# Cached attention beside a small feed-forward on one core: a weight block loaded a round later, half of the last V in the key buffers, and the products of two heads moved ahead of the last maximum

## The chip, the cores and the metric

The kernel runs on one core of a Trainium2 chip. The metric is the device time of one execution in microseconds, the median of several. Five engines run side by side and meet only at semaphores: TensorE (PE in the profile), VectorE (DVE), ScalarE (ACT), GpSimd (POOL, nearly unused here) and SyncE (SP), which here does nothing but issue transfers from DRAM to the on-chip memory. A transfer that SP issues must first wait until its destination buffer is free, and SP issues in program order: while it waits, every later transfer waits behind it.

## The reference

Two rows of input x (B = 2, D = 448) go through two branches, which are mixed by a gate. Everything is f32.

```python
g = sigmoid((x * gate_w).sum(-1))
q = (x @ wq)                                  # 16 heads of 256, one query row per batch entry
p = softmax(q . k_cache * 256 ** -0.5)        # 4096 keys for each head and batch entry
a = (p @ v_cache) @ wo                        # back to 448
h = relu(x @ w1 + b1) ** 2                    # 1792 wide
b = h @ w2 + b2
out = g * a + (1 - g) * b
```

Nearly all bytes are k_cache and v_cache, 134 MB each. The weights are wq 7.3 MB, wo 7.3 MB, w1 and w2 3.2 MB each. Each byte is used once.

## The kernel before

**Rounds.** The 32 pairs of a batch entry and a head are worked off in 16 rounds, `rounds[i] = (b, n)` (L129): round i takes batch entry b and the two heads 2n and 2n+1, 64 partitions for each head, 64 keys in each partition. Round 15 is the last. Heads 12 and 13 are rounds 12 and 13, heads 14 and 15 are rounds 14 and 15.

**Buffers.** There are three ring buffers of 4.2 MB (`slot`, L69) and one wide buffer of 8.4 MB (`wide_slot`, L72). A round's keys come in two halves, each in a ring buffer (`load_k`, L138; the text calls the halves k5_0 and k5_1 for round 5). A round's values fill the wide buffer (`load_v`, L144; v5 for round 5). Weight blocks take a whole ring buffer, however small they are: w1 in round 1, the first two chunks of w2 (`load_w2_early`, 0.46 MB), the four groups of wo (`load_wo`, 1.84 MB each; called wo0 to wo3) and the other twelve chunks of w2 (`load_w2_late`, 2.75 MB in four pieces).

**What a round does.** DVE multiplies the half of the keys by the query in place (`times_q`, L295) and adds up along the head (`row_sums`, L300), for both halves; `rest(i)` is that for all but the first 16 columns. Then comes the round's maximum (L304, turned across partitions by a product on PE, L308, and read back at L314), ACT takes the exponentials (L319), and PE multiplies them with V (`values`, L345, 64 matmuls a round). While PE does this, DVE is already at the next round's keys.

**What sets the order.** It is the order of the program, engine by engine (`manual_schedule`, L67). SP's issues stand at the head of each round: the round's V, then weight blocks, then the second half of the next round's keys and the first half of those after it (L423 to L438). V waits for the wide buffer, that is for the end of the products of the round before. A ring buffer comes free when `row_sums` has read a half of keys, or when the last product with a weight block is done.

**Units of heads.** Four heads share an accumulator. When a unit is done (rounds 3, 7 and 11), its sum is read by ACT (`take`, L355), turned by PE (`turn`, L373) and multiplied with its group of wo (`project`, L386); round 3 also multiplies the two early chunks of w2 (L464). The last four heads form two units of two heads. Their products with wo3 (`late_wo`, L394) and those with the late chunks of w2 (`late_w2`, L398) go into a second accumulator, all through the helper at L391.

**The end.** In the last round V comes in four pieces (`V_CUTS`), and PE multiplies each as it lands; the `late_wo` of heads 12 and 13 stand between these pieces (L477 to L483). Then follow `take` and `turn` of the last unit, the late chunks of w2 and heads 14 and 15, one reading by ACT (L491) and two small stores.

Of the kernel before, what the change touches and what calls it, by code (L numbers as in the profile page):

```python
# [16 lines left out]
def kernel(  # L17
# [14 lines left out]
    nc = tc.nc  # L32
    P = 128
    B, H, S, DH = k_cache.shape
# [7 lines left out]
    NK = S // PH  # L42
    J = NK // 2
# [8 lines left out]
    DQ = D // 4  # L52
    WH = 2
    W2_CUTS = (4, 8, 11)
    V_CUTS = (32, 48, 56)
    LEAD = 4
    LEAD2 = 16
    scale = DH ** -0.5
# [10 lines left out]
    def slot(name):  # L69
        return ring.tile([P, J * DH], F32, name=name, tag="ring")  # L70

    def wide_slot(name):  # L72
        return wide.tile([P, NK * DH], F32, name=name, tag="wide")
# [10 lines left out]
    def load_w1():  # L84
        t = slot("w1")[:, :D * F // P]
        nc.sync.dma_start(t, w1.rearrange("(r k) (s n) -> (r k s) n", k=XR, s=2).rearrange(
            "(p k) n -> p (k n)", k=XR))
        return t
# [11 lines left out]
    def load_w2_early():  # L100
        tv = w2_slot(0, WH)
        nc.sync.dma_start(tv, w2_v[:, :WH, :])

    def load_w2_late():
        tv = w2_slot(WH, FC)
        at = [0, *W2_CUTS, FC - WH]
        for lo, hi in zip(at, at[1:]):
            nc.sync.dma_start(tv[:, lo:hi, :], w2_v[:, WH + lo:WH + hi, :])  # L108
# [9 lines left out]
    def load_wo(g):  # L118
        t = slot(f"wo{g}")
        tv = t[:, :HJ * D]  # L120
        if g < NG - 1:
            nc.sync.dma_start(tv, wo_g[g])
            wo_sb[g] = tv.rearrange("p (j n) -> p j n", j=HJ)
        else:
            nc.sync.dma_start(tv.rearrange("p (h k) -> p h k", h=HG), wo_v[:, g * HG:(g + 1) * HG, :])
            wo_sb[g] = tv.rearrange("p (h j n) -> p h j n", h=HG, j=NJ)
# [3 lines left out]
    last = len(rounds) - 1  # L130

    def of_round(src, i):
        b, n = rounds[i]
        return src[b, 2 * n:2 * n + 2].rearrange("h (p j) d -> (h p) j d", p=PH)
# [3 lines left out]
    def load_k(i, half):  # L138

        t = slot(f"k{i}_{half}").rearrange("p (j d) -> p j d", d=DH)  # L140
        nc.sync.dma_start(t, of_round(k_cache, i)[:, half * J:(half + 1) * J, :])
        kts[i, half] = t

    def load_v(i, cuts=()):  # L144
        t = wide_slot(f"v{i}").rearrange("p (j d) -> p j d", d=DH)
        at = [0, *cuts, NK]
        for lo, hi in zip(at, at[1:]):
            nc.sync.dma_start(t[:, lo:hi, :], of_round(v_cache, i)[:, lo:hi, :])  # L148
        return t


    wq_t = load_wq()
# [139 lines left out]
    def times_q(i, half, lo, hi):  # L292

        kt = kts[i, half][:, lo:hi, :]
        nc.vector.tensor_tensor(kt, kt, q_sb[i].unsqueeze(1).to_broadcast([P, hi - lo, DH]), op=ALU.mult)  # L295

    def row_sums(i, half):
        if half == 0:
            s_t[i] = work.tile([P, NK], F32, name=f"s{i}", tag="s")
        nc.vector.tensor_reduce(s_t[i][:, half * J:(half + 1) * J], kts[i, half], axis=AX.X, op=ALU.add)  # L300

    def maximum(i):
        m = work.tile([P, 1], F32, name=f"m{i}", tag="m")
        nc.vector.tensor_reduce(m, s_t[i], axis=AX.X, op=ALU.max)  # L304
        mt = ps.tile([P, 512], F32, name=f"mt{i}", tag="sm")
        for k in range(2):
            at = slice(k * PH, (k + 1) * PH)
            nc.tensor.matmul(mt[at, :PH], m.to_broadcast([P, PH]), ident[:, at], start=True, stop=True)  # L308
        return mt

    def softmax(i, mt):
        b, n = rounds[i]
        nb = work.tile([P, 1], F32, name=f"nb{i}", tag="nb")
        nc.vector.tensor_reduce(nb, mt[:, :PH], axis=AX.X, op=ALU.max, negate=True)  # L314
        u, k = unit_of[2 * n]
        for e in range(2):
            at = slice(e * PH, (e + 1) * PH)
            c = B * (k + e) + b
            nc.scalar.activation(pw[k, b][at, :, 2 * c:2 * c + 2], s_t[i][at].rearrange("p (m s) -> p m s", s=2), AF.Exp,  # L319
                                 bias=nb[at], accum_out=rs_t[u % 2][at, c:c + 1])  # L320

    def sums(u):
        sm = ps.tile([P, 512], F32, name=f"sum{u}", tag="sm")
        n = B * len(units[u])
        nc.tensor.matmul(sm[:, :n], ones_pp, rs_t[u % 2][:, :n], start=True, stop=True)  # L325
        return sm

    def norm(u, sm):
        n = len(units[u])
        rc = work.tile([P, n, B], F32, name=f"rc{u}", tag="rc")  # L330
        nc.vector.reciprocal(rc, sm[:, :B * n].rearrange("p (k b) -> p k b", b=B))
        nc.vector.tensor_tensor(rc, rc, gP[:, 0, :].unsqueeze(1).to_broadcast([P, n, B]), op=ALU.mult)
        rl = work.tile([P, n * B, 2], F32, name=f"rl{u}", tag="rl")
        nc.vector.tensor_tensor(rl, m16[:, :4 * n].rearrange("p (c s) -> p c s", s=2),
                                rc.rearrange("p k b -> p (k b)").unsqueeze(2).to_broadcast([P, n * B, 2]), op=ALU.mult)
        rl_t[u] = rl

    def values(i, vt, lo=0, hi=NK // 2):
        b, h = rounds[i]
        u, k = unit_of[2 * h]  # L340
        n = len(units[u])
        po = po_bufs[u % 2]
        for m in range(lo, hi):
            r = 32 * (m % 4)
            nc.tensor.matmul(po[r:r + 4 * n, :], pw[k, b][:, m, :4 * n], vt[:, 2 * m:2 * m + 2, :].rearrange("p j d -> p (j d)"),  # L345
                             start=(k == 0 and b == 0 and m < 4), stop=(k == n - 2 and b == B - 1 and m >= NK // 2 - 4))
# [37 lines left out]
    def project(g):  # L384
        for j in range(HJ):
            nc.tensor.matmul(acc[:, :D], oT[g][:, j, :], wo_sb[g][:, j, :], start=False,  # L386
                             stop=(g == NG - 2 and j == HJ - 1))

    def late(lt, rhs, start=False, stop=False):
        for k in range(4):  # L390
            nc.tensor.matmul(fin[32 * k:32 * k + B, :DQ], lt, rhs[:, k * DQ:(k + 1) * DQ], start=start, stop=stop)  # L391

    def late_wo(h):
        u, k = unit_of[h]  # L394
        for j in range(NJ):
            late(oT[u][:, j, B * k:B * k + B], wo_sb[NG - 1][:, h % HG, j, :])
# [13 lines left out]
    def rest(i):  # L410
        times_q(i, 0, LEAD2, J)
        row_sums(i, 0)
        times_q(i, 1, 0, J)
        row_sums(i, 1)
# [3 lines left out]
    for i, (b, n) in enumerate(rounds):  # L418
        u, k = unit_of[2 * n]
        done = b == B - 1 and k == len(units[u]) - 2  # L420


        vt = load_v(i, V_CUTS if i == last else ())  # L423
        if i == 1:
            w1_t = load_w1()
        if i == 3:
            load_w2_early()
        if done and u < NG - 1:
            load_wo(u)
        if i == last - 1:  # L430
            load_wo(NG - 1)
        if i == last:
            load_w2_late()
        if i < last - 1:
            load_k(i + 1, 1)
            load_k(i + 2, 0)
        if i == last - 2:
            load_k(last, 1)  # L438

        mt = maximum(i)  # L440
        if i < last:
            times_q(i + 1, 0, 0, LEAD)
        softmax(i, mt)
        if i < last:
            times_q(i + 1, 0, LEAD, LEAD2)
        if done:
            norm(u, sums(u))
        if i == last:
            break
        values(i, vt)  # L450


        if done:
            take(u)
            turn(u)
            if u < NG - 1:
                project(u)
        if i == 1:
            ffn_hidden(w1_t)
        if i == 2:  # L460
            pt = ffn_turn()
        if i == 3:
            for c in range(WH):
                nc.tensor.matmul(acc[:, :D], hT[:, c, :], w2_sb[c], start=False, stop=False)  # L464
        if i + 2 <= last:
            make_q(i + 2)
        if i == last - 3:

            ya = const.tile([B, D], F32, name="ya")
            nc.scalar.activation(ya, acc[:, :D], AF.Copy)  # L470
            late(ident[:B, :B], ya, start=True)
        rest(i + 1)
        if i == 2:
            ffn_square(pt)


    p1, p2, p3 = (c // 2 for c in V_CUTS)  # L477
    values(last, vt, 0, p1)
    values(last, vt, p1, p2)
    late_wo(H - 4)  # L480
    values(last, vt, p2, p3)
    late_wo(H - 3)
    values(last, vt, p3, NK // 2)  # L483
    take(NG)
    turn(NG)
    late_w2(0, W2_CUTS[0])
# [35 lines left out]
```

## Time and profile before

| what | value |
|---|---|
| median of 3 runs | 702.95 us (702.36 to 703.0) |
| the profiled execution's own time | 703.78 us |
| its span, first to last instruction | 702.0 us |
| bytes read from DRAM | 289.56 MB, 412 GB/s over the span |
| DVE busy | 571.9 us (81%) |
| PE busy | 240.4 us (34%) |
| granted TensorE clock, mean | 0.653 |

The span lies 1.78 us below the profiled execution's own time, which in turn lies 0.83 us above the median of the runs. In the profile, one row of the timeline is a group of like instructions: its start, its duration, the engine, the line, and in brackets the idle time of the engine before it and what ended it. A row of the chain of waits is a link of the chain that ended last: start, duration, and what took it; for a transfer it runs from the issue to the landing. A row of the windows gives, for a stretch of the span, the busy time of PE, of its weight loads (PEld), of DVE, ACT and POOL, then the granted clock, the busy share of the DMA engines and the GB/s that they moved.

### The profile page before, as it was taken

To read this page: it belongs to the slowest core of one execution; us is meant where nothing else is said; L and a number is where in the kernel's file an instruction comes from. 1 tells how busy PE (TensorE), PEld (TensorE's weight loads), DVE (VectorE), ACT (ScalarE), POOL (GpSimd) and SP (SyncE) were. 2 spreads that over 40 slices of the span, in tenths; PEclk is the share of its full clock that TensorE was granted. 3 is DMA by queue.
4 is the path that set the end of the run, shared out by engine and by line. 5 is a ranking of instruction groups with operands and counts; after the bars stand their busy time and mean duration, and the time that the engine had idled before them with its cause. 6 is when DMAs were issued, how large, how long until landed. Compare 5 with 4: busy or idle time off the path is not lost.

```text
span 702.0 us, 3763 instructions
## 1 busy us (share of the span) xinstructions
PE 240.4 (34%) x1618; PEld 82.8 (12%) x1618; DVE 571.9 (81%) x171; ACT 35.5 (5%) x110; POOL 0.7 (0%) x6
## 2 busy tenths in 40 slices
PE   2501408018086050321407440230507532240436
PEld 1100102004041010000103110000103100010013
DVE  3299997897948929979895989989795998989940
ACT  0100000100010000000001000000001000000000
POOL 0000000000000000000000000000000000000000
PEclk9955757656567565565757666565757657575678
DMA  9999999999975999999989999999999999999786
GB/s 413 399 444 422 471 418 415 429 436 450 399 311 209 418 445 448 390 451 415 474 388 434 471 395 446 420 439 428 440 437 420 441 426 433 429 426 447 300 361 275
DMA packets 9500, 289.79 MB, mean 413 GB/s; under 512 B 1158, under 2 KB 1292, under 8 KB 2316
## 3 DMA queue, kind: packets, MB, share of 16 engines
q1 hardware_dynamic: 9320, 289.54, 96.2%
q8 instruction: 12, 0.20, 0.1%
q10 hardware_dynamic: 164, 0.02, 0.0%
q14 instruction: 4, 0.03, 0.0%
HBM read 289.56 MB, written 0.00 MB: 412 GB/s over the span
## 4 chain that ended last, share of the span: by engine, by line
DMA 65%; PE 20%; DVE 12%; ACT 1%; SPq 0%; issue 0%; ACTq 0%
DMA v<-in_A_v_cache_dram 59%; PE po_buf L345 17%; DVE k L295 6%; DVE s L300 6%; DMA w<-in_B_w_dram 4%; DMA wq<-in_A_wq_dram 3%; PE po_buf L215 1%; PE acc L386 1%; PE ot L373 1%; ACT shared L355 0%; SPq L148 0%; PE fin L391 0%; SPq L108 0%; ACT oT L379 0%; PE pq L252 0%
## 5 line engine op out<-in xcount | busy, mean ns | idle before, releaser
L295 DVE TENSOR_TENSOR k<-k,q 128x4096 f32<-128x4096 f32 (+3 forms) x63 | 281.7, 4487 | 95.2 <-DMA k<-in_A_k_cache_dram 76.6
L300 DVE TENSOR_REDUCE s<-k 128x32 f32<-128x8192 f32 x32 | 278.0, 8686 | 1.1
L345 PE MATMUL po_buf<-v,pw 128*16 128x512 f32 (+1 forms) x1024 | 145.5, 730 | 166.1 <-DMA v<-in_A_v_cache_dram 166.1
L308 PE MATMUL mt<-ident,m 128*64 128x64 f32 x64 | 7.7, 335 | 256.4 <-DVE m L304 256.4
L345 PEld LDWEIGHTS po_buf<-v,pw 128*16 128x16 f32 (+1 forms) x1024 | 32.2, 110 | 265.7 <-issue 225.3
L308 PEld LDWEIGHTS mt<-ident,m 128*64 128x64 f32 x64 | 5.1, 204 | 263.9 <-issue 220.7
L319 ACT ACTIVATE pw<-s,nb 64x64 f32<-64x64 f32 x32 | 11.2, 349 | 295.6 <-DVE nb L314 295.2
L386 PE MATMUL acc<-wo,oT 128*2 128x448 f32 x48 | 24.3, 671 | 2.5 <-ACT oT L379 2.5
L373 PE MATMUL ot<-rl,shared 128*128 128x8 f32 x96 | 16.1, 305 | 5.2 <-ACT shared L355 5.2
L255 ACT ACTIVATE q<-pq 128x256 f32<-128x256 f32 x16 | 6.1, 384 | 209.9 <-PE pq L252 209.8
L373 PEld LDWEIGHTS ot<-rl,shared 128*128 128x128 f32 x96 | 15.6, 254 | 8.3 <-ACT shared L355 8.3
L252 PE MATMUL pq<-qs,ident 128*64 128x256 f32 x64 | 10.7, 419 | 0.7 <-ACT qs L241 0.7
L215 PE MATMUL po_buf<-wq,xT 128*4 128x512 f32 x56 | 8.1, 741 | 4.7 <-DMA wq<-in_A_wq_dram 4.7
L355 ACT ACTIVATE shared<-po_buf 128x1024 f32<-128x1024 f32 x6 | 5.8, 1021 | 53.5 <-PE po_buf L345 53.5
L276 PEld LDWEIGHTS pt<-ident,shared 4*128 4x128 f32 x28 | 6.9, 336 | 0.9 <-issue 0.9
L276 PE MATMUL pt<-ident,shared 4*128 4x4 f32 x28 | 7.0, 380 | 0.0
L386 PEld LDWEIGHTS acc<-wo,oT 128*2 128x2 f32 x48 | 4.4, 97 | 20.1 <-issue 17.3
L319 ACT ACTIVATION_READ_ACCUMULATOR pw<-s,nb 64x1 f32 x32 | 5.9, 185 | 0.0
L325 PE MATMUL sum<-rs,ones_pp 128*128 128x8 f32 (+1 forms) x10 | 3.0, 368 | 8.1 <-ACT pw L319 8.1
L215 PE MATMUL ph<-w,xT 128*4 128x448 f32 x28 | 5.4, 539 | 0.0
L252 PEld LDWEIGHTS pq<-qs,ident 128*64 128x64 f32 x64 | 3.3, 138 | 11.7 <-issue 9.8
L314 DVE TENSOR_REDUCE nb<-mt 128x1 f32<-128x64 f32 x16 | 3.5, 218 | 0.7 <-PE mt L308 0.7
(60 smaller groups left out, 54.8 us busy)
## 6 DMA issues: line engine op xcount, KB each, us to landing
k<-in_A_k_cache_dram SPq DMA_DIRECT2D x32, 4096.0 KB, 31.0
wq<-in_A_wq_dram SPq DMA_DIRECT2D x1, 7168.0 KB, 19.5
wo<-in_A_wo_dram SPq DMA_DIRECT2D x4, 1792.0 KB, 29.5
v<-in_A_v_cache_dram SPq DMA_DIRECT2D x1, 4096.0 KB
w<-in_B_w_dram SPq DMA_DIRECT2D x1, 3136.0 KB, 33.2
v<-in_A_v_cache_dram SPq DMA_DIRECT2D x1, 2048.0 KB
v<-in_A_v_cache_dram SPq DMA_DIRECT2D x2, 1024.0 KB, 19.6
w<-in_B_w_dram SPq DMA_DIRECT2D x2, 896.0 KB, 23.0
```

The costliest lines, as they stand in the source:

```text
L215: nc.tensor.matmul(out[32 * g:32 * g + 2 * B, :width], xT[:, half, c].rearrange("p s b -> p (s b)"), t[:, (a * n + g) * width:(a * n + g + ...
L252: nc.tensor.matmul(pq[k * PH:(k + 1) * PH, :DH], ident[:, r:r + 1].to_broadcast([P, PH]), qs[:, k * DH:(k + 1) * DH], start=True, stop=True)
L255: nc.scalar.activation(q_sb[i], pq[:, :DH], AF.Copy)
L276: nc.tensor.matmul(pt[:, c, :], hv[:, c, :], ident[:2 * B, :2 * B], start=True, stop=True)
L295: nc.vector.tensor_tensor(kt, kt, q_sb[i].unsqueeze(1).to_broadcast([P, hi - lo, DH]), op=ALU.mult)
L300: nc.vector.tensor_reduce(s_t[i][:, half * J:(half + 1) * J], kts[i, half], axis=AX.X, op=ALU.add)
L308: nc.tensor.matmul(mt[at, :PH], m.to_broadcast([P, PH]), ident[:, at], start=True, stop=True)
L319: nc.scalar.activation(pw[k, b][at, :, 2 * c:2 * c + 2], s_t[i][at].rearrange("p (m s) -> p m s", s=2), AF.Exp, bias=nb[at], accum_out=rs_ ...
L345: nc.tensor.matmul(po[r:r + 4 * n, :], pw[k, b][:, m, :4 * n], vt[:, 2 * m:2 * m + 2, :].rearrange("p j d -> p (j d)"), start=(k == 0 and ...
L355: nc.scalar.activation(o_w[:, s], po_bufs[u % 2][:, s * DH:(s + 1) * DH].rearrange("r (p j) -> r j p", j=HJ).unsqueeze(2).to_broadcast([P, ...
L373: nc.tensor.matmul(ptv[:, j, :], ov[:, s, j, :], rl_t[u][:, :, s], start=(s == 0), stop=(s == 1))
L386: nc.tensor.matmul(acc[:, :D], oT[g][:, j, :], wo_sb[g][:, j, :], start=False, stop=(g == NG - 2 and j == HJ - 1))
```

## The change

Three things change.

1. `load_w2_early` and the products of its two chunks move from round 3 to round 4. In round 3 wo0 now follows V directly.
2. The last V is loaded by a function of its own. Its first half goes into a ring buffer (`va`), its second half into the second half of the wide buffer (`vb`), in pieces of 16, 8 and 8 columns. As a buffer of the ring goes to `va`, the late chunks of w2 get the next one.
3. The `late_wo` of heads 12 and 13 move from between the pieces of the last V to the end of round 14's products, ahead of the last round's row sums and maximum in the program.

```diff
-    V_CUTS = (32, 48, 56)
+    V_CUTS = (48, 56)
...
-    def load_v(i, cuts=()):
+    def load_v(i):
         t = wide_slot(f"v{i}").rearrange("p (j d) -> p j d", d=DH)
-        at = [0, *cuts, NK]
+        nc.sync.dma_start(t, of_round(v_cache, i))
+        return t
+
+    def load_v_last():
+
+        ta = slot("va").rearrange("p (j d) -> p j d", d=DH)
+        nc.sync.dma_start(ta, of_round(v_cache, last)[:, :J, :])
+        tb_ = wide_slot("vb").rearrange("p (j d) -> p j d", d=DH)
+        at = [J, *V_CUTS, NK]
         for lo, hi in zip(at, at[1:]):
-            nc.sync.dma_start(t[:, lo:hi, :], of_round(v_cache, i)[:, lo:hi, :])
-        return t
+            nc.sync.dma_start(tb_[:, lo:hi, :], of_round(v_cache, last)[:, lo:hi, :])
+        return ta, tb_
...
-        vt = load_v(i, V_CUTS if i == last else ())
+        vt = load_v_last() if i == last else load_v(i)
         if i == 1:
             w1_t = load_w1()
-        if i == 3:
+        if i == 4:
             load_w2_early()
...
-        if i == 3:
+        if i == 4:
             for c in range(WH):
                 nc.tensor.matmul(acc[:, :D], hT[:, c, :], w2_sb[c], start=False, stop=False)
...
+        if i == last - 1:
+            late_wo(H - 4)
+            late_wo(H - 3)
         rest(i + 1)
...
-    p1, p2, p3 = (c // 2 for c in V_CUTS)
-    values(last, vt, 0, p1)
-    values(last, vt, p1, p2)
-    late_wo(H - 4)
-    values(last, vt, p2, p3)
-    late_wo(H - 3)
-    values(last, vt, p3, NK // 2)
+    p2, p3 = (c // 2 for c in V_CUTS)
+    values(last, vt[0], 0, J // 2)
+    values(last, vt[1], J // 2, p2)
+    values(last, vt[1], p2, p3)
+    values(last, vt[1], p3, NK // 2)
```

SP's row of issues from round 3's V on, with what each waits for, before: v_414 is v3, w_0_416 the early block of w2, wo_418 is wo0, k_1_420 and k_0_422 are k4_1 and k5_0, v_518 is v4, k_1_520 and k_0_522 are k5_1 and k6_0. A DMAHW entry is a wait for an earlier transfer, PE and DVE are waits for those engines.

```order
-L148 DMA v_414<-in_A_v_cache_dram 128x16384 [waits DMAHW7_49,PE_49]
-L102 DMA w_0_416<-in_B_w_dram 128x896 [waits DMAHW6_49,DVE_49]
-L122 DMA wo_418<-in_A_wo_dram 128x3584 [waits DVE_49]
-L141 DMA k_1_420<-in_A_k_cache_dram 128x8192 [waits DMAHW5_49,DMAHW1_49,DVE_49]
-L141 DMA k_0_422<-in_A_k_cache_dram 128x8192 [waits DMAHW4_49,PE_49]
-L148 DMA v_518<-in_A_v_cache_dram 128x16384 [waits DMAHW2_49]
-L141 DMA k_1_520<-in_A_k_cache_dram 128x8192 [waits DMAHW3_49,DMAHW0_49,PE_49]
-L141 DMA k_0_522<-in_A_k_cache_dram 128x8192 [waits DVE_49]
```

The same stretch now, where wo_416 is wo0, k_1_418 and k_0_420 are k4_1 and k5_0, v_514 is v4, w_0_516 the early block of w2, k_1_518 and k_0_520 are k5_1 and k6_0.

```order
+L146 DMA v_414<-in_A_v_cache_dram 128x16384 [waits DMAHW7_49,PE_49]
+L122 DMA wo_416<-in_A_wo_dram 128x3584 [waits DMAHW6_49,DVE_49]
+L141 DMA k_1_418<-in_A_k_cache_dram 128x8192 [waits DVE_49]
+L141 DMA k_0_420<-in_A_k_cache_dram 128x8192 [waits DMAHW5_49,DMAHW1_49,DVE_49]
+L146 DMA v_514<-in_A_v_cache_dram 128x16384 [waits DMAHW2_49,PE_49]
+L102 DMA w_0_516<-in_B_w_dram 128x896 [waits DMAHW3_49,PE_49]
+L141 DMA k_1_518<-in_A_k_cache_dram 128x8192 [waits DMAHW0_49,DVE_49]
+L141 DMA k_0_520<-in_A_k_cache_dram 128x8192 [waits DMAHW5_49,DVE_49]
```

wo0 takes the place of the early block, each of the two halves of keys behind it moves one buffer up, and k5_0's wait for PE becomes a wait for DVE. The early block now stands behind v4 and waits for PE, in wo0's buffer.

SP's last issues before: v_1214 is v14, wo_1216 is wo3, v_1266 is the last V, w_2_1271 the late chunks of w2.

```order
-L148 DMA v_1214<-in_A_v_cache_dram 128x16384 [waits DMAHW4_49,PE_49]
-L125 DMA wo_1216<-in_A_wo_dram 128x4x896 [waits DVE_49]
-L148 DMA v_1266<-in_A_v_cache_dram 128x8192 [waits DMAHW2_49,DMAHW0_49,PE_49]
-L148 DMA v_1266<-in_A_v_cache_dram 128x4096
-L148 DMA v_1266<-in_A_v_cache_dram 128x2048
-L148 DMA v_1266<-in_A_v_cache_dram 128x2048 [waits DMAHW5_49]
-L108 DMA w_2_1271<-in_B_w_dram 128x1792 [waits DMAHW6_49,DVE_49]
```

The same issues now.

```order
+L146 DMA v_1214<-in_A_v_cache_dram 128x16384 [waits DMAHW4_49,PE_49]
+L125 DMA wo_1216<-in_A_wo_dram 128x4x896 [waits DVE_49]
+L152 DMA va<-in_A_v_cache_dram 128x8192 [waits DMAHW6_49,DMAHW2_49,DVE_49]
+L156 DMA vb<-in_A_v_cache_dram 128x4096 [waits DMAHW0_49,PE_49]
+L156 DMA vb<-in_A_v_cache_dram 128x2048
+L156 DMA vb<-in_A_v_cache_dram 128x2048 [waits DMAHW5_49]
+L108 DMA w_2_1288<-in_B_w_dram 128x1792 [waits DVE_49]
```

The first half of the last V waits for DVE (the row sums of k15_0) and no longer for PE; the second half waits for PE, as the whole did; the late chunks of w2 have a wait for DVE as before, now for the row sums of k15_1.

PE's row from round 14's products on, before: mt_1278 is the last maximum, sum_1285 the last unit's sums, pw_1_101 holds the exponentials.

```order
-L345 MATMUL po_buf_92<-v_1214,pw_0_99 8x512 x32
-L308 MATMUL mt_1278<-ident,m_1276 64x64 x2
-L325 MATMUL sum_1285<-rs_107,ones_pp 128x4
-L345 MATMUL po_buf_92<-v_1266,pw_1_101 8x512 x24
-L391 MATMUL fin<-wo_1216,oT_1202 2x112 x8
-L345 MATMUL po_buf_92<-v_1266,pw_1_101 8x512 x4
-L391 MATMUL fin<-wo_1216,oT_1202 2x112 x8
-L345 MATMUL po_buf_92<-v_1266,pw_1_101 8x512 x4
-L373 MATMUL ot_1342<-rl_1290,o_1340 128x4 x4
```

The same stretch now, with mt_1295 the last maximum.

```order
+L353 MATMUL po_buf_92<-v_1214,pw_0_99 8x512 x32
+L399 MATMUL fin<-wo_1216,oT_1202 2x112 x16
+L316 MATMUL mt_1295<-ident,m_1293 64x64 x2
+L333 MATMUL sum_1302<-rs_107,ones_pp 128x4
+L353 MATMUL po_buf_92<-va,pw_1_101 8x512 x16
+L353 MATMUL po_buf_92<-vb,pw_1_101 8x512 x16
+L381 MATMUL ot_1343<-rl_1307,o_1341 128x4 x4
```

The sixteen products of heads 12 and 13 (the profile counts each product of the program as two matmuls) move from between the pieces of V to the place ahead of the last maximum.

## Prediction

> **What bounds the kernel now.** I read the page first: busy shares, the slices of the DMA engines and the chain that ended last.
>
> ```profile
> PE 240.4 (34%) x1618; PEld 82.8 (12%) x1618; DVE 571.9 (81%) x171; ACT 35.5 (5%) x110; POOL 0.7 (0%) x6
> DMA  9999999999975999999989999999999999999786
> GB/s 413 399 444 422 471 418 415 429 436 450 399 311 209 418 445 448 390 451 415 474 388 434 471 395 446 420 439 428 440 437 420 441 426 433 429 426 447 300 361 275
> DMA v<-in_A_v_cache_dram 59%; PE po_buf L345 17%; DVE k L295 6%; DVE s L300 6%; DMA w<-in_B_w_dram 4%; DMA wq<-in_A_wq_dram 3%; PE po_buf L215 1%; PE acc L386 1%; PE ot L373 1%; ACT shared L355 0%; SPq L148 0%; PE fin L391 0%; SPq L108 0%; ACT oT L379 0%; PE pq L252 0%
> ```
>
> The transfers are the bound: 59% of the chain is V landing, and the DMA engines are full except in slices 11 and 12 (about 193 to 228 us) and in the last three. So I asked for the windows around those two places, and one long window between them.
>
> ```profile
> 193.70:251.50 57.80, 26.32 (x124) 10.97 (x124) 42.92 (x9) 3.90 (x11) 0.00 (x0) 0.65 0.78 326
> 197.50:202.50 5.00, 5.00 (x48) 1.12 (x40) 3.88 (x1) 0.00 (x0) 0.00 (x0) 0.92 0.23 73
> 212.50:220.00 7.50, 7.45 (x17) 1.57 (x18) 6.63 (x1) 0.00 (x1) 0.00 (x0) 0.81 0.00 0
> 251.50:291.80 40.30, 10.43 (x72) 2.70 (x72) 29.02 (x8) 1.26 (x5) 0.00 (x0) 0.63 1.00 429
> 262.50:655.00 392.50, 121.29 (x770) 37.90 (x770) 351.77 (x89) 18.68 (x64) 0.00 (x0) 0.63 1.00 432
> 655.00:662.50 7.50, 2.76 (x16) 0.64 (x20) 7.50 (x2) 0.00 (x0) 0.00 (x0) 0.50 0.85 345
> 662.50:667.50 5.00, 5.00 (x48) 1.14 (x44) 4.96 (x2) 0.00 (x0) 0.00 (x0) 1.00 0.09 36
> 667.50:672.50 5.00, 0.62 (x8) 0.00 (x0) 5.00 (x1) 0.00 (x0) 0.00 (x0) 1.00 0.76 282
> ```
>
> From 262.5 to 655 us the DMA share is 1.00 at 432 GB/s, and DVE works 351.77 of 392.50 us, so it has a tenth to spare. Whatever removes an idle microsecond of the DMA engines ahead of that stretch moves all of it forward. At 432 GB/s half of a round's keys (4.194 MB) takes 9.71 us and the early w2 block (0.459 MB) 1.06.
>
> The chain in order of time shows the rounds; a row is one V, from issue to landing.
>
> ```profile
> 164.95 28.77 DMA v<-in_A_v_cache_dram
> ...
> 220.50 30.96 DMA v<-in_A_v_cache_dram
> ...
> 261.02 30.74 DMA v<-in_A_v_cache_dram
> ...
> 339.95 29.64 DMA v<-in_A_v_cache_dram
> ...
> 378.08 34.80 DMA v<-in_A_v_cache_dram
> ...
> 421.94 29.72 DMA v<-in_A_v_cache_dram
> ...
> 620.00 39.61 DMA v<-in_A_v_cache_dram
> ```
>
> v3 lands at 193.72, v4 at 251.46, v5 at 291.76, v7 at 369.59, v8 at 412.88, v9 at 451.66, v14 at 659.61. A full round with a block of wo (v7 to v8) takes 43.29 us, one without (v8 to v9) 38.78; v3 to v4 took 57.74. Why, SP's issues show.
>
> ```profile
> 165.37 0.38 SPq L102 DMA_DIRECT2D w<-in_B_w_dram  x1
> 182.09 0.33 SPq L122 DMA_DIRECT2D wo<-in_A_wo_dram  x1
> 201.41 19.04 SPq L141 DMA_DIRECT2D k<-in_A_k_cache_dram  x2
> 220.50 0.42 SPq L148 DMA_DIRECT2D v<-in_A_v_cache_dram  x1
> ...
> 638.28 0.39 SPq L125 DMA_DIRECT2D wo<-in_A_wo_dram  x1
> 668.19 1.87 SPq L148 DMA_DIRECT2D v<-in_A_v_cache_dram  x4
> ```
>
> Two small blocks hold two of the three ring buffers. k4_1 is issued at 201.41 when k4_0 has been read, and k5_0, the second of that row, at 220.12 (201.41 + 19.04, less the 0.33 of its issue), when `project(0)` gives wo0's buffer back; v4 stands behind it. Between them the queue runs dry twice, and DVE and PE show what ended the waits.
>
> ```profile
> 192.69 8.69 DVE L300 TENSOR_REDUCE s<-k 128x32 f32<-128x8192 f32 x1
> 213.37 8.69 DVE L295 TENSOR_TENSOR k<-k,q 128x8192 f32<-128x8192 f32 x1 [11.99 <-DMA k<-in_A_k_cache_dram]
> ...
> 383.83 8.69 DVE L295 TENSOR_TENSOR k<-k,q 128x8192 f32<-128x8192 f32 x1 [7.50 <-DMA k<-in_A_k_cache_dram]
> ...
> 410.40 8.69 DVE L300 TENSOR_REDUCE s<-k 128x32 f32<-128x8192 f32 x1
> ```
>
> ```profile
> 212.56 7.53 PE L386 MATMUL acc<-wo,oT 128*2 128x448 f32 x16 [0.82 <-ACT oT L379]
> 219.93 1.67 PE L464 MATMUL acc<-w,hT 128*2 128x448 f32 x4
> ```
>
> **Part 1, the early w2 block a round later.** In round 3, wo0 is now issued in w2's place at 165.4; k4_1 takes the buffer of k3_1, where wo0 was issued at 182.09; k5_0 waits for k4_0's row sums, 192.69 + 8.69 = 201.38. v4 then waits only for its buffer, released when v3's products end; in rounds 4 and 7 such products end 9.56 and 8.49 us after the landing (261.02 - 251.46, 378.08 - 369.59), so about 203. Both dry spells go: behind v3 stand wo0, k4_1, k5_0 and v4, the same queue as in rounds 7 and 8. I take that round's 43.29 us: v4 lands at 237.0.
>
> Round 4 now holds the small block. It waits for `project(0)`, which ends at 212.56 + 7.53 = 220.1, and SP's next issues stand behind it: k5_1, k6_0, then v5. None is late for the engines, which are busy until v4 lands at 237.0. k5_1 waits for the row sums of k4_1: that half lands 14.24 us after v3, as k8_1 did after v7 (383.83 - 369.59), so at 208.0, and two DVE passes of 8.69 end at 225.4. k6_0 waits for the row sums of k5_0: in round 8 these end 410.40 + 8.69 - 369.59 = 49.5 us after v7's landing, so at 243.2 here. The queue lasts until v4 (237.0), the block (1.06) and k5_1 (9.71) are through, at 247.8. An issue took 11.96 us to land a half on an empty queue (201.41 to 213.37), 2.25 over its 9.71, so k6_0 has some 2.3 us to spare. The four products of the block (1.67 us) run after v4's products, near 248; k6_1 waits for them, and its turn comes only after v5, near 277. So round 4 costs 38.78 + 1.06, and v5 lands at 193.72 + 43.29 + 39.84 = 276.85, against 291.76: **14.9 us earlier**. Rounds 5 to 14 keep their pattern, since each issue hangs on V's products or on row sums, which hang on landings.
>
> The windows give the bounds. Counting only the two emptiest, 7.50 x (1 - 0/432) + 5.00 x (1 - 73/432) = 11.7 us. Counting all from 193.70 to 291.80, 57.80 x (1 - 326/432) + 40.30 x (1 - 429/432) = 14.5. I take 14.9, since a round of the same queue was measured, and keep 11.7 as the low end.
>
> On the small block a rule of the Trainium skill speaks against the move: the page "SBUF — State Buffer", section "The DMA setup-cost knee", gives every transfer a roughly fixed 2 us beside its bytes. By it the block between two large transfers would cost some 3 us instead of 1.06, and the gain would be 12.9. The trace agrees for a transfer on an empty queue (2.25 us above), but not behind others: wo1's 1.835 MB made its round 43.29 - 38.78 = 4.51 us longer, 0.26 over the 4.25 of its bytes.
>
> **Part 2, half of the last V in the ring.** The rows of the end, of DVE and of PE:
>
> ```profile
> 647.40 8.69 DVE L300 TENSOR_REDUCE s<-k 128x32 f32<-128x8192 f32 x1
> ...
> 664.72 8.69 DVE L300 TENSOR_REDUCE s<-k 128x32 f32<-128x8192 f32 x1
> ```
>
> ```profile
> 673.81 0.48 PE L308 MATMUL mt<-ident,m 128*64 128x64 f32 x4 [5.69 <-DVE m L304]
> 675.60 0.59 PE L325 MATMUL sum<-rs,ones_pp 128*128 128x4 f32 x2 [1.31 <-ACT pw L319]
> 680.28 6.80 PE L345 MATMUL po_buf<-v,pw 128*8 128x512 f32 x48 [4.09 <-DMA v<-in_A_v_cache_dram]
> 686.89 0.57 PE L391 MATMUL fin<-wo,oT 128*2 128x112 f32 x16
> ...
> 690.13 1.04 PE L345 MATMUL po_buf<-v,pw 128*8 128x512 f32 x8 [1.05 <-DMA v<-in_A_v_cache_dram]
> ...
> 697.67 0.95 PE L391 MATMUL fin<-w,hT 128*2 128x112 f32 x32 [0.60 <-DMA w<-in_B_w_dram]
> ```
>
> All times here are on the clock of before; the 14.9 comes off later. The last V is issued at 668.19, when v14's products end, and its first half lands at 680.28, with the DMA engines nearly idle from 662.5 on. Now `va` waits for k15_0's row sums, 647.40 + 8.69 = 656.1, and stands in the queue before v14 and wo3 are through. By the row of k8_1 behind a wo block, it lands 14.24 us after v14: 673.85, **6.4 us earlier**. `vb` is issued at 668.19 with the last V's old release, 5.7 us ahead of `va`'s landing, so the queue stays filled; its pieces land as before 9.85 us after the first half (690.13 - 680.28), the last at 683.7. The late w2 chunks now wait for k15_1's row sums, 664.72 + 8.69 = 673.4, some 10 us ahead of their turn, and land 7.54 us after V (697.67 - 690.13), at 691.24.
>
> PE can follow. The exponentials are ready at 675.6 as before, and now they are what PE waits for. From 676.2 (675.60 + 0.59) it has 32 matmuls for `va`; 48 took 6.80 us with a slow start, and the last 16 of them, at 1.04 for 8, make 2.1, so the 32 take 4.7: 680.9. At 1.04 for 8 the first piece of `vb` ends at 683.0, the second at 684.0 and the last, which lands at 683.7, at 685.0; to keep step with V it would be 691.17 - 6.4 = 684.8. What follows V's last product took from 691.17 to the last wait, at 697.07 (697.67 - 0.60), 5.9 us: 690.9, against w2's 691.24. So PE costs nothing, or a few tenths if its slow start is longer. Bounds of this part from the windows: 5.00 x (1 - 36/432) = 4.6 us for the emptiest stretch alone; with 1.5 of the row before and 1.7 of the row behind it, 7.8. I take 6.4, which rests on landings.
>
> **Part 3, products of heads 12 and 13.** 32 matmuls, in two groups of 16 with 0.57 us each, leave the places between V's pieces, where PE was waiting for V anyway (0.20 and 1.05 us of idle): nothing gained by itself. They now run at 668.2, ahead of the last maximum, in a wait of 5.69 us for DVE. wo3 has landed by then (v14 at 659.61, and 4.25 for its bytes). Cost nothing; without that cover 1.1 us would fall on the maximum, the exponentials and the last V's products.
>
> **How the numbers follow.** 14.9 + 6.4 = 21.3 us. The profiled execution has a span of 702.0 and its own time of 703.78, so it would come to 682.5; the median of the runs is 0.83 lower, 702.95 - 21.3 = **681.6 us**. Its own bounds: 702.95 - 14.9 - 7.8 = 680.2, and 702.95 - 11.7 - 4.6 = 686.7. About 0.2% (1.4 us) is what a measurement here can tell from no change.
>
> **Rivals.**
>
> - *The dry spell moves to round 4* (8%). The ring loses a buffer to a small block in two rounds running, and k6_0 has only 2.3 us to spare. If it is later than that, the queue empties once more, at worst like the 7.5 us of 212.5 to 220: 689.1. Against it: k4_1, on which k6_0's release hangs, stands in the same queue, so if it lands late the queue lasts longer too.
> - *The end is not bound by V* (6%). If the last row sums, the exponentials or the late w2 chunks decide, the 6.4 us go: 688.1. Against it: PE idles 4.09 us ahead of 680.28 and 1.05 ahead of 690.13, both put down to V, and w2's release has 10 us to spare. For it: those 4.09 us are less than 6.4, so the exponentials, not `va`, start the products.
> - *The small block costs its fixed time* (4%): 2 us more in round 4, worked out from the 2.25 us of an empty queue, 683.6. It is the case of the Trainium skill's page above.
> - *Slower than before* (2%). SP's queue is the mechanism: the block, waiting for `project(0)` in round 4, holds k5_1, k6_0 and v5 behind it. It costs nothing until `project(0)` ends after 234.7 (237.0 less 2.3), then one for one; to eat 21.3 us and 1.4 more it must end after 257, 37 us later than in the trace. Then 704.4 or more. Nothing in the trace points there.
> - *The queue isn't the bound, and filling it does nothing* (1%): 703.0. The 432 GB/s over 392 us speak against it.
>
> My forecast keeps 79%. The range is its bounds, 680.0 to 686.7, and leaves out the outer rivals. Faster 0.97, the same 0.01, slower 0.02.
>
> **What would show it.** Right, if slices 11 and 12 stand above 400 GB/s, v4 lands near 237 and v5 near 277, SP issues two halves of keys near 182 and 201, the window from v14's landing to the last V's has no empty stretch, and PE's first product of the last V is released by ACT's exponentials. Wrong, if a gap shows between 237 and 260, if `va` lands over 15 us after v14, or if PE's last wait is no longer for w2.

## The result, and the profile after

The changed kernel takes 682.39 us in the median of 4 runs (682.0 to 683.37), the kernel before 702.98 (702.36 to 703.88): a ratio of 0.9708, with a 95% interval of 0.9691 to 0.9725, or some 20.6 us. The forecast was 681.6, with a range of 680.0 to 686.7.

The page of the changed kernel, with the lines that answer to those of before: busy times, the slices of the DMA engines, the chain that ended last.

```profile
PE 242.7 (36%) x1618; PEld 83.6 (12%) x1618; DVE 571.7 (84%) x171; ACT 35.4 (5%) x110; POOL 0.7 (0%) x6
DMA  9999999999999999999999999999999999999996
GB/s 378 435 458 419 430 456 410 453 410 427 456 397 454 415 447 439 411 456 412 450 407 433 442 420 442 425 444 423 443 435 413 450 414 452 413 431 451 400 409 251
DMA v<-in_A_v_cache_dram 51%; PE po_buf L353 15%; DVE k L303 10%; DVE s L308 10%; DMA k<-in_A_k_cache_dram 6%; DMA wq<-in_A_wq_dram 3%; DMA w<-in_B_w_dram 2%; PE po_buf L223 1%; PE fin L399 0%; PE pq L260 0%; ACT qs L249 0%; SPq L108 0%; DVE nb L322 0%; ACT q L263 0%; SPq L141 0%
```

The work of the engines is nearly the same (DVE 571.7 us against 571.9, PE 242.7 against 240.4); the dips in slices 11 and 12 and near the end are gone, and the DMA engines are full up to the last slice. The windows of the changed kernel, at the places where the kernel before ran dry:

```profile
193.70:237.10 43.40, 25.53 (x120) 10.32 (x120) 36.96 (x9) 3.89 (x11) 0.00 (x0) 0.66 1.01 434
237.10:277.00 39.90, 11.34 (x76) 3.00 (x76) 35.13 (x9) 1.26 (x5) 0.00 (x0) 0.63 1.00 431
277.00:640.00 363.00, 122.40 (x766) 39.46 (x766) 321.52 (x82) 17.78 (x60) 0.00 (x0) 0.64 1.00 433
640.00:650.00 10.00, 4.07 (x20) 0.79 (x24) 10.00 (x2) 0.00 (x0) 0.00 (x0) 0.50 0.96 397
650.00:660.00 10.00, 5.90 (x81) 1.90 (x73) 9.78 (x3) 0.00 (x0) 0.00 (x0) 0.98 0.97 398
660.00:672.50 12.50, 10.47 (x70) 2.56 (x70) 0.74 (x4) 1.47 (x5) 0.00 (x0) 0.73 0.99 411
```

Rounds 3 and 4 move 434 and 431 GB/s, where the window of round 3 stood at 326. From 640 to 672.5 us the DMA share stays at 0.96 or above, where it fell to 0.09. One of the prediction's signs is missed by a hair: slice 11 stands at 397 GB/s, not above 400 (slice 12 at 454). Single slices, the last left aside, jump between 378 and 458 here, and the window over that place shows no gap.

The chain of waits of the changed kernel, V by V:

```profile
203.95 33.08 DMA v<-in_A_v_cache_dram
...
246.02 30.90 DMA v<-in_A_v_cache_dram
...
364.44 33.25 DMA v<-in_A_v_cache_dram
...
484.60 29.83 DMA v<-in_A_v_cache_dram
...
522.92 35.30 DMA v<-in_A_v_cache_dram
```

v4 lands at 237.03 and v5 at 276.92; the forecast had 237.0 and 276.85. v8 lands at 397.69, 15.2 us earlier than before. SP's issues, round 3 and 4 and the end:

```profile
164.53 0.38 SPq L122 DMA_DIRECT2D wo<-in_A_wo_dram  x1
182.32 19.64 SPq L141 DMA_DIRECT2D k<-in_A_k_cache_dram  x2
203.95 0.33 SPq L146 DMA_DIRECT2D v<-in_A_v_cache_dram  x1
221.03 0.33 SPq L102 DMA_DIRECT2D w<-in_B_w_dram  x1
225.38 18.17 SPq L141 DMA_DIRECT2D k<-in_A_k_cache_dram  x2
...
642.30 0.34 SPq L152 DMA_DIRECT2D va<-in_A_v_cache_dram  x1
655.20 1.28 SPq L156 DMA_DIRECT2D vb<-in_A_v_cache_dram  x3
659.62 1.80 SPq L108 DMA_DIRECT2D w<-in_B_w_dram  x4
```

k4_1 and k5_0 go out at 182.3 and 201.6 (182.32 + 19.64, less 0.33), v4 at 203.95 instead of 220.50. `va` is issued 12.9 us ahead of `vb`, before v14 has landed. PE's rows of the end:

```profile
645.93 9.20 PE L353 MATMUL po_buf<-v,pw 128*8 128x512 f32 x64 [20.61 <-DMA v<-in_A_v_cache_dram]
654.95 0.94 PE L399 MATMUL fin<-wo,oT 128*2 128x112 f32 x32
660.00 0.34 PE L316 MATMUL mt<-ident,m 128*64 128x64 f32 x4 [4.10 <-DVE m L312]
661.64 0.59 PE L333 MATMUL sum<-rs,ones_pp 128*128 128x4 f32 x2 [1.31 <-ACT pw L327]
662.16 6.18 PE L353 MATMUL po_buf<-va,pw 128*8 128x512 f32 x32
668.17 3.61 PE L353 MATMUL po_buf<-vb,pw 128*8 128x512 f32 x32
...
673.54 0.95 PE L399 MATMUL fin<-w,hT 128*2 128x112 f32 x32
...
677.15 0.95 PE L399 MATMUL fin<-w,hT 128*2 128x112 f32 x32 [1.13 <-DMA w<-in_B_w_dram]
```

There is no bracket at 662.16 and 668.17: PE starts the last V when the exponentials are there and never waits for V again. The products of heads 12 and 13 (654.95) end four microseconds before the last maximum. What ends last is w2, for which PE waits 1.13 us.

One line of the page could mislead. The chain's DVE share has grown from 12% to some 20%, since it now runs through the last row sums, which release the late w2 chunks at 659.6. But those transfers then lay in a full queue behind `vb` (the DMA share from 660 to 672.5 us is 0.99), so an earlier release would hardly have brought them sooner; no run tried it.

### The profile page after: what moved, and what is told of

It is laid out like the page before. It is cut to its first block, busy times and chain, and to the rows that moved or that the text cites. A ratio compares the mean times of both kernels' runs of the same rounds, so it can differ in the third digit from the quotient of the medians.

```text
span 681.5 us, 3765 instructions
## 1 busy us (share of the span) xinstructions
PE 242.7 (36%) x1618; PEld 83.6 (12%) x1618; DVE 571.7 (84%) x171; ACT 35.4 (5%) x110; POOL 0.7 (0%) x6
## 4 chain that ended last, share of the span: by engine, by line
DMA 62%; DVE 21%; PE 16%; issue 0%; ACT 0%; SPq 0%
DMA v<-in_A_v_cache_dram 51%; PE po_buf L353 15%; DVE k L303 10%; DVE s L308 10%; DMA k<-in_A_k_cache_dram 6%; DMA wq<-in_A_wq_dram 3%; DMA w<-in_B_w_dram 2%; PE po_buf L223 1%; PE fin L399 0%; PE pq L260 0%; ACT qs L249 0%; SPq L108 0%; DVE nb L322 0%; ACT q L263 0%; SPq L141 0%
## 5 line engine op out<-in xcount | busy, mean ns | idle before, releaser
L353 PE MATMUL po_buf<-v,pw 128*16 128x512 f32 (+1 forms) x960 | 137.7, 738 | 150.6 <-DMA v<-in_A_v_cache_dram 150.6
L381 PE MATMUL ot<-rl,shared 128*128 128x8 f32 x96 | 17.7, 322 | 5.2 <-ACT shared L363 5.2
L381 PEld LDWEIGHTS ot<-rl,shared 128*128 128x128 f32 x96 | 17.2, 278 | 8.3 <-ACT shared L363 8.3
L353 PE MATMUL po_buf<-va,pw 128*8 128x512 f32 x32 | 6.2, 947 | 0.0
```

The source lines that it names most:

```text
L381: nc.tensor.matmul(ptv[:, j, :], ov[:, s, j, :], rl_t[u][:, :, s], start=(s == 0), stop=(s == 1))
```

## The experiments

The kernel before was measured again beside the experiments: 704.07 us (701.51 to 705.45) beside the first four and 703.73 (701.84 to 705.38) beside the last four. So the ratios to it count more than the differences of medians.

**Part 1 alone.**

```diff
-        if i == 3:
+        if i == 4:
             load_w2_early()
...
-        if i == 3:
+        if i == 4:
             for c in range(WH):
```

> The kernel before with part 1 alone: the early w2 block and its products go from round 3 to round 4; the last V and the products of heads 12 and 13 stay as they were. Theory (the DMA queue is the bound, and what the ring buffer held back in round 3 is all of this part's gain): v4 near 237, v5 near 277, and the end as in the kernel before, so 14.9 us less: 688.1, between 687.4 and 689.0. Rival (round 4 pays for the block with a dry spell of its own that the other parts hide): over 690. Rival (the gain needs part 2 to reach the end): over 695.

Measured: 691.63 us, a ratio of 0.9828 (0.9805 to 0.985), some 12.1 us less; 2.6 us above the theory's upper end, and above the first rival's 690. The profile does not bear the rival out: v5's products start at 277.03, as in the changed kernel, and v14's at 645.89, against 645.93. Over half of what is missing is lost behind v14. PE's rows there:

```profile
645.89 9.57 PE L345 MATMUL po_buf<-v,pw 128*8 128x512 f32 x64 [20.60 <-DMA v<-in_A_v_cache_dram]
...
667.57 7.25 PE L345 MATMUL po_buf<-v,pw 128*8 128x512 f32 x48 [5.22 <-DMA v<-in_A_v_cache_dram]
...
684.93 1.53 PE L391 MATMUL fin<-w,hT 128*2 128x112 f32 x32 [0.53 <-DMA w<-in_B_w_dram]
```

And its window over v14's products:

```profile
645.90:655.50 9.60, 9.56 (x64) 1.88 (x64) 9.56 (x2) 0.00 (x0) 0.00 (x0) 0.73 0.20 79
```

The queue is nearly dry at 79 GB/s while PE works on v14. And the same 64 matmuls took 9.57 us in this run (granted clock 0.73), not the 8.38 of the kernel before, whose window over its own products shows a clock of 0.84:

```profile
659.70:668.20 8.50, 8.38 (x64) 1.78 (x64) 8.46 (x2) 0.00 (x0) 0.00 (x0) 0.84 0.38 146
```

The last V waits for them, so from v14's first product to the last wait for w2 it is 39.0 us instead of 37.9. The last 32 matmuls took 1.53 us instead of 0.95, and from that wait on it is 0.4 us more. Together that is some 1.5 us, and 1.1 more had been given back before v14 (below): the spans differ by 702.0 - 689.7 = 12.3 us, 2.6 less than the 14.9.

**Part 2 alone.** The changed kernel's `load_v_last`, with the early block in round 3 and the products of heads 12 and 13 between the pieces of V:

```diff
+    def load_v_last():
+        ta = slot("va").rearrange("p (j d) -> p j d", d=DH)
...
-        vt = load_v(i, V_CUTS if i == last else ())
+        vt = load_v_last() if i == last else load_v(i)
```

> The kernel before with part 2 alone: half of the last V in the ring; the early w2 block stays in round 3, the products of heads 12 and 13 between the pieces of V. Theory: the DMA engines no longer run dry behind wo3, 6.4 us less: 696.6, between 695.8 and 697.4. Rival (the end hangs on the last row sums, the exponentials and the late w2 chunks): under 2 us less, above 701.

Measured: 696.41 us, a ratio of 0.9895 (0.9875 to 0.9914), 7.4 us less. PE's rows of its end:

```profile
660.08 8.78 PE L353 MATMUL po_buf<-v,pw 128*8 128x512 f32 x64 [20.62 <-DMA v<-in_A_v_cache_dram]
...
676.45 5.70 PE L353 MATMUL po_buf<-va,pw 128*8 128x512 f32 x32
...
691.50 0.95 PE L399 MATMUL fin<-w,hT 128*2 128x112 f32 x32 [0.91 <-DMA w<-in_B_w_dram]
```

v14 stands where it stood (660.08 against 659.74), and from there to the last wait for w2 it is 31.4 us instead of 37.9: 6.5 of the forecast 6.4. The rival, an end that hangs on DVE's last row sums, is out. The two parts add up: 0.9828 x 0.9895 = 0.9725, at the upper edge of the interval of the whole change.

**Part 3 alone.**

```diff
+        if i == last - 1:
+            late_wo(H - 4)
+            late_wo(H - 3)
         rest(i + 1)
...
-    late_wo(H - 4)
     values(last, vt, p2, p3)
-    late_wo(H - 3)
     values(last, vt, p3, NK // 2)
```

> The kernel before with part 3 alone: the products of heads 12 and 13 ahead of the last maximum. Theory: they leave places where PE waited for V and enter a wait for DVE, so nothing moves: 703.0, within 0.6. Rival (PE's work between the pieces of V set the end): 1.1 us less, 701.9.

Measured: 703.36 us, a ratio of 1.0005 (0.9988 to 1.0022): nothing, as forecast.

**The change without part 3.**

```diff
-        if i == last - 1:
-            late_wo(H - 4)
-            late_wo(H - 3)
         rest(i + 1)
...
+    late_wo(H - 4)
     values(last, vt[1], p2, p3)
+    late_wo(H - 3)
     values(last, vt[1], p3, NK // 2)
```

> The changed kernel without part 3: the products of heads 12 and 13 stand between the pieces of the last V again. In the changed kernel PE runs through the last V without a wait for it, and later waits 1.13 us for w2. Theory: the 0.9 us of these products fit into that wait, 682.4 to 682.7. Rival (PE from the exponentials on sets the end, so that part 3 carries some of the gain): 1 us or more longer, 683.4 and above.

Measured: 682.41 us, a ratio of 0.9696 (0.9675 to 0.9716), the same as the change. PE's last rows:

```profile
671.28 1.03 PE L353 MATMUL po_buf<-vb,pw 128*8 128x512 f32 x8
...
675.61 1.72 PE L399 MATMUL fin<-w,hT 128*2 128x112 f32 x64
```

The last product of V now ends at 672.3 instead of 671.8, and the late w2 products run through without a wait: the products of heads 12 and 13 have filled PE's idle time ahead of w2, and no more. So part 3 is worth nothing either way, but here PE has no slack left.

**The early block in round 3, in a buffer of its own.** The kernel before with this edit alone; it tells the ring buffer from the block's transfer and place.

```diff
-        tv = w2_slot(0, WH)
+        tv = const.tile([P, WH, D], F32, name="w2_own")
+        for c in range(WH):
+            w2_sb[c] = tv[:, c, :]
         nc.sync.dma_start(tv, w2_v[:, :WH, :])
```

> The kernel before, where the early w2 block stays in round 3, ahead of wo0, but lies in a small buffer of its own and takes none from the ring. Theory (what costs is the ring buffer that the small block holds, not its transfer or its place in SP's row): wo0, k4_1 and k5_0 wait as in the changed kernel, v4 lands near 238, v5 near 277, and the time is that of part 1 alone, 691.6, between 690 and 693. Rival (the block must leave round 3, because its transfer or its issue ahead of wo0 holds the row up): 700 or more.

Measured: 690.35 us, a ratio of 0.9822 (0.9801 to 0.9844), as part 1 alone. SP's issues in round 3:

```profile
165.26 0.43 SPq L104 DMA_DIRECT2D w_own<-in_B_w_dram  x1
165.78 0.38 SPq L124 DMA_DIRECT2D wo<-in_A_wo_dram  x1
182.14 19.64 SPq L143 DMA_DIRECT2D k<-in_A_k_cache_dram  x2
203.03 0.33 SPq L150 DMA_DIRECT2D v<-in_A_v_cache_dram  x1
```

The block is issued where it always was, ahead of wo0, and the halves of keys go out at 182 and 201 and v4 at 203 all the same; v4 lands at 237.96 and v5 at 276.76. So what cost 12 to 13 us was 0.46 MB holding a 4.2 MB buffer, not its transfer and not its place in SP's row.

**Two small blocks in round 7.** The changed kernel with `i == 7` in both places of part 1, so that the early block stands ahead of wo1 as it had stood ahead of wo0.

```diff
-        if i == 4:
+        if i == 7:
             load_w2_early()
...
-        if i == 4:
+        if i == 7:
             for c in range(WH):
```

> The changed kernel with the early w2 block and its products in round 7, ahead of wo1, as the kernel before had them in round 3 ahead of wo0. Theory (two small blocks in one round make the queue run dry, in whichever round): k8_1 waits for k8_0's row sums, k9_0 for the end of project(1) some 24 us after v7's landing, v8 lands 11 us later than with one block, and the time is 693.4, between 692 and 697. Rival (the dry spell belonged to round 3, where DVE is still ahead of its data and the hidden layer is turned): 682.4 to 684.

Measured: 696.1 us (693.98 to 697.24), a ratio of 0.9893 (0.9868 to 0.9919). SP's issues from wo1 on, and three windows:

```profile
341.70 0.33 SPq L122 DMA_DIRECT2D wo<-in_A_wo_dram  x1
360.07 20.13 SPq L141 DMA_DIRECT2D k<-in_A_k_cache_dram  x2
380.26 0.42 SPq L146 DMA_DIRECT2D v<-in_A_v_cache_dram  x1
```

```profile
355.00:360.00 5.00, 5.00 (x38) 1.12 (x34) 5.00 (x1) 0.00 (x0) 0.00 (x0) 0.69 0.40 167
370.00:375.00 5.00, 4.18 (x11) 1.80 (x12) 2.80 (x1) 0.70 (x4) 0.00 (x0) 0.50 0.23 98
375.00:380.00 5.00, 5.00 (x14) 1.11 (x13) 5.00 (x1) 0.00 (x0) 0.00 (x0) 0.99 0.00 0
```

The same two dry spells, now between 356 and 361 and from 371 to 380, with v8 queued behind a half of keys that waits for `project(1)`. So it is the second small block in a round, not something of round 3. It costs 13 us by the ratios (13.7 by the medians), more than the 11 expected. `project(1)` ended 26.5 us after v7's landing, not 24. The 24 match round 7 of the kernel before (393.5 - 369.6 = 23.9). Here v7's products took 9.4 us instead of 8.4, and `turn` 6.6 instead of 4.4: the granted clock was 0.50 all through it, where the kernel before had 0.76 in the window of 380 to 385 us. (The products of `project(1)` gave 0.6 us of that back.)

**V in four transfers.** The changed kernel, with 45 transfers more of the same bytes.

```diff
-        nc.sync.dma_start(t, of_round(v_cache, i))
+        for lo in range(0, NK, NK // 4):
+            nc.sync.dma_start(t[:, lo:lo + NK // 4, :], of_round(v_cache, i)[:, lo:lo + NK // 4, :])
```

> The changed kernel, where V of rounds 0 to 14 comes in four transfers instead of one: 45 transfers more of the same bytes. PE can start on a quarter and so frees the wide buffer some 6 us sooner after V's landing. Theory (the queue is always filled, so neither a transfer's fixed time nor an earlier release counts): 682.4, within 1. Rival (each transfer costs its fixed time of some 2 us behind others too): 45 times 2, above 750; or a tenth of that, 691. Rival (V's release sets the rounds): under 680.

Measured: 685.58 us (685.38 to 685.94), a ratio of 0.9748 (0.9727 to 0.9768), 3.2 us more than the change (2.8 by the ratios). From its page:

```profile
GB/s 377 441 422 439 431 417 442 419 437 430 420 434 424 432 430 424 436 424 435 425 431 437 419 439 420 439 423 437 427 423 434 423 436 425 432 435 423 418 429 270
DMA packets 15980, 289.80 MB, mean 424 GB/s; under 512 B 1878, under 2 KB 2012, under 8 KB 3036
```

The queue stays full. If all 3.2 us are theirs, the 45 transfers cost 0.07 us each, far from 2. Buffers that come free sooner bring no gain that shows either; the run holds both effects at once and gives only their sum. The expectation of no more than 1 us was missed by 2. There are 15980 packets, not 9500, and the loss builds up over the whole span (a mean of 424 GB/s against 425); why is not shown.

**The change with the early block in a buffer of its own.** The same edit as in the fifth experiment, on the changed kernel.

> The changed kernel, where the early w2 block of round 4 lies in a small buffer of its own. It tells whether the block still costs something in the ring, where k6_0 had 2.3 us to spare by the prediction. Theory: nothing is late in round 4, 682.4, within 0.6. Rival (the block in the ring still holds up rounds 4 and 5): 1 us less or more, 681.4 and below.

Measured: 682.13 us (681.84 to 682.39), a ratio of 0.9698 (0.9678 to 0.9718): the same as the change. In round 4 the block's buffer costs nothing.

## Why the prediction was right

- **What bounds the kernel.** Right: filling the queue moved everything behind it. The spans differ by 702.0 - 681.5 = 20.5 us, with the same bytes and nearly the same engine work.
- **Part 1.** Right in its mechanism, shown by the block in its own buffer (no dry spell) and by the two blocks in round 7 (the dry spell again). Up to v5 also right in size: 291.76 - 276.92 = 14.8 us against 14.9. k6_0 was in time too: it was issued at 243.2 (225.38 + 18.17, less 0.33), as forecast, and 431 GB/s in that window show no gap.
- **"Rounds 5 to 14 keep their pattern."** Nearly. v14's products start at 645.93 instead of 659.74: 13.8 us remain of 14.9. Most of what is missing went in round 11, from v11 to v12: 43.79 us after the change (514.43 to 558.22), 43.07 before, by these two rows of the chain of the kernel before:

```profile
499.97 29.26 DMA v<-in_A_v_cache_dram
...
538.11 34.19 DMA v<-in_A_v_cache_dram
```

  In part 1 alone, without part 3 and in both kernels with an own buffer that round also took 43.7 to 44.4 us between the starts of V's products; in part 2 alone, part 3 alone and with two blocks in round 7, 43.2. So it goes with reaching that round 14 to 15 us earlier. In both kernels no stretch of 5 us in it is empty (the DMA share is 0.85 or above), so no wait of an engine shows as its cause. What lowers the rate there stays open.
- **Part 2.** Right: 6.7 us from v14 to the last wait for w2 (37.9 to 31.2), against 6.4, and 6.5 in part 2 alone. Part 1 alone showed a side of it that was not in the prediction: with the whole last V behind v14's products, the end hangs on how fast PE does them. From the start of these products to the last wait for w2 it was 37.9 us where they took 8.38 (the kernel before), 37.8 where they took 8.46 (the block in its own buffer) and 39.0 where they took 9.57 (part 1 alone). With half of the last V in the ring it was 31.4 us with 8.78 (part 2 alone), 31.2 with 9.20 (the change) and 30.1 with 9.90 (two blocks in round 7): slower products no longer lengthen it. What makes the 1.3 us between these three stays open. One sign of the prediction can't be read: when `va` landed. PE never waited for it, so the trace says only that it was there at 662.16, 16.2 us after v14's products began.
- **PE after the last maximum.** Its terms were off, both ways. 4.7 us were given to `va`'s 32 matmuls, and 6.0 it was (662.16 to 668.17). In both kernels the granted clock stood at 0.50 when the last V's products began, but here it stayed there longer. The second window of these products, in the kernel before and in the changed one:

```profile
682.50:685.00 2.50, 2.50 (x24) 0.46 (x16) 0.00 (x0) 0.00 (x0) 0.00 (x0) 0.91 0.96 410
```

```profile
665.00:667.50 2.50, 2.50 (x16) 0.47 (x12) 0.00 (x0) 0.00 (x0) 0.00 (x0) 0.53 1.00 422
```

  `vb`'s 32 then took 3.61, less than the 4.1 given to them. What follows V took 4.2 us (671.78 to 676.02), not 5.9: the clock stayed at 1.00, and 32 late products took 0.95 where they had taken 1.42 to 1.74. The clocks of that stretch, in the window of the kernel before and in that of the changed one:

```profile
692.50:695.00 2.50, 2.50 (x57) 2.32 (x60) 0.00 (x0) 0.18 (x1) 0.00 (x0) 0.64 1.01 413
```

```profile
672.50:675.00 2.50, 2.50 (x72) 2.48 (x76) 0.00 (x0) 0.18 (x1) 0.00 (x0) 1.00 0.73 286
```

  So PE came to its last wait 30.1 us after v14's products had begun, where 31.2 were forecast (690.9 - 659.74). The forecast had left PE only 0.3 us ahead of w2 there, so it is partly luck that these errors cost nothing: they cancelled in part, and w2 set the end.

  The clock dropped as PE's wait of 4.10 us ended: it was 1.00 from 657.5 to 660, 0.61 from 660 to 662.5 and 0.50 from there to 665. On that the Trainium skill, "TensorE: Matmul & The Clock Gate", section "What's actually happening", says that an idle window of about 3.4 us brings the clock back to half; the 4.10 us agree.
- **The products of heads 12 and 13.** Right: nothing, alone or within the change.
- **The rivals.** None came about with its price. Of "the end is not bound by V" the conditions came true in part: the exponentials start the last V's products, and the late w2 chunks are what PE waits for last. But w2 stands behind V in the same full queue, so the 6.4 us did not go. The rival on a transfer's fixed time was tested by itself. The Trainium skill's 2 us a transfer ("SBUF — State Buffer", "The DMA setup-cost knee") would, by an estimate from that figure, have made V in quarters 90 us longer if each were paid in the queue. It became 3.2 us longer: here the 2 us show for a transfer on an empty queue (2.25 us over its bytes), not behind others.

So 21.3 us were forecast and 20.6 measured; the 1.1 us given back in the late rounds are the difference, less 0.3 more than forecast at the end.

## What to carry to other kernels

When transfers are the bound, look at what each buffer holds, not only at what each transfer moves: a small block in a large buffer of a ring takes as much lead as a full one, and two of them between the same two large loads can empty the queue, as 0.46 MB did here for 12 to 13 us. Spread such blocks over rounds or give them buffers of their own; and let the last large load begin in a buffer that comes free early, so that it doesn't wait for the compute on the one before. Where the queue was always full, moved products brought nothing here, earlier releases nothing that shows, and 45 more transfers 3 us. So look for the dry spells first.

## What the runs showed of the hardware

A transfer behind others paid almost nothing for itself: at most 0.07 us for each of 45 more, against 2.25 us over its bytes on an empty queue (201.41 to 213.37 us in the kernel before). A filled queue moved 424 to 438 GB/s in stretches of 80 to 108 us of the kernel before and of the changed one, and 432 and 433 in the longest windows, of 392 and 363 us. And the 64 matmuls on v14 took 8.4 to 9.9 us from run to run (8.38 at a granted clock of 0.84, 9.57 at 0.73). That moved the end where the whole last V waited for them, and not where half of it lay in the ring.
